# Attention scores and gate logits: one 4-byte product of unsplit operands for three products of split halves

## The chip, the cores and the metric

The kernel runs on one core of a Trainium2 chip, in one launch. The metric is the device time of that launch in microseconds (us). Three timed runs of the kernel before gave 884.1, 889.33 and 892.63 us; the median is 889.33 us. One further run was profiled and took 885.66 us.

The engines are called by the profile's names: PE is TensorE (PEld its loads of weights, the stationary operand), DVE is VectorE, ACT is ScalarE, POOL is GpSimd and SP is SyncE. Each engine takes its instructions in the order in which they were written for it.

## The reference

Three layers follow one another: causal attention with a window of 128 positions and a bias linear in the distance (batch 4, 8 heads, 576 positions, head size 64), a mixture of 8 experts in which each token goes to the one expert with the largest logit, and a gated layer. All of it is in 4-byte floating point.

```python
scores = q @ k.T / sqrt(64)                       # per batch and head
scores = where(0 <= rel < 128, scores - slope[h] * abs(rel), -1e9)
attn = softmax(scores);  x = (attn @ v).reshape(2304, 512)
logits = x @ w_gate + modality_bias[modality_id]  # (2304, 8)
e = argmax(logits);  gate = softmax(logits)[e]
x = gate * (relu(x @ w1[e]) @ w2[e])
xn = x / rms(x) * rms_g
out = (silu(xn @ w_gate2) * (xn @ w_val)) @ w_out
```

The change touches two products: the scores `q @ k.T` and the logits `x @ w_gate`. Which expert a token goes to hangs on the logits' largest entry.

## The kernel before, in words

**Tiles and stages.** The 2304 tokens are 18 tiles of 128. The attention stage, with the gate, fills the first 200 us or so of the span; the expert layer and the gated layer follow, are mostly large products, and are not touched by the change.

**The attention pipeline.** A tile `t` has two half tiles `g`, of four heads each. `attention_step(n)` writes out one step of a pipeline over half tiles: it goes through the table `AT` (lines 800 to 806), whose entries are a name and a lag, and writes the named piece of work for the half tile `n - lag`. The order of the table is therefore the order of each engine's queue; there is no scheduler that moves anything. There are 36 score groups (`qk`), one for each half tile, and the distance from one group to the next is called a step here. Pieces that exist once for a tile are written in every second step.

**The split of scores.** For each tile, `tq` and `tk` transpose q and k on PE (line 180, four transposes of 128x128 each) into a PSUM bank (pool bank "d", two of them). `qhi` and `khi` copy the bank on ACT into `qT[:, 0]` and `kT[:, 0]`, of type F32R, in which a product is one pass with rounded operands (lines 198 and 211). `qlo` and `klo` then write on DVE what the rounding took off, into `qT[:, 1]` and `kT[:, 1]` (lines 202 and 215). `kT` is a ring of three tiles, and the scores of a tile go against its own 128 keys and the 128 before it: 256 columns, or 128 at the start of a batch that begins with a tile (tiles 0 and 9).

**The score products.** `qk` (lines 226 to 251) has two products of heads side by side: head `j = 0` lies in rows 0 to 63 of the operands, head `j = 1` in rows 64 to 127, each with its own PSUM bank (bank "a"). For each of two pairs of heads (`u`) it issues high by high, high by low and low by high, 12 products in a group:

```python
for u in range(2):
    for n, (ql, kl) in enumerate(((0, 0), (0, 1), (1, 0))):
        for j in range(2):
            nc.tensor.matmul(sps[j][:, u, :W], qT[rows, ql, i], win(kl, i, j), ...)
```

`ttr` (line 278, DVE) adds the bias and takes the row's extreme, `exp` (line 289, ACT) the exponential, and in the next step `pt` transposes the result on PE (lines 311 and 319), `pall` and `pcur` copy it (lines 325 and 331 or 334), and a step later `pv` multiplies it by v (lines 354 and 356). The operands of `pv` are F32, not split; in the trace each of its products is recorded as two loads of weights and two matmuls.

**The gate.** `xs` (line 366, DVE) scales a tile's output, `tx` transposes it (line 375), `xhi` (line 380, ACT) and `xlo` (line 385, DVE) split it, and `lg` (lines 391 and 392) issues eight F32R products with the split gate weights `wgr` as the stationary operand and 128 columns. `lT` (line 396, ACT) copies the result, `tl` (line 400, one F32 product with the constant `two`) adds its two halves and turns it, and `gate` (line 407 onward, DVE) reads the logits from the bank `few`. `route`, `place` and an indirect DMA by POOL (line 455, `xd<-xs,pli`) then put the tile's rows in the order of the experts.

**Other work in the stage.** POOL and ACT split the weights of the two largest experts (lines 577 and 578) in the later steps. `choose` (line 459) picks these two experts after tile 4, on DVE.

Of the kernel before, what the change touches and what calls it, by code (L numbers as in the profile page):

```python
# [8 lines left out]
F32 = mybir.dt.float32  # L9
F32R = mybir.dt.float32r  # L10
# [4 lines left out]
AF = mybir.ActivationFunctionType  # L15
ALU = mybir.AluOpType
# [3 lines left out]
P = 128  # L20
B, H, SEQ, DH = 4, 8, 576, 64
# [3 lines left out]
KD = D // P  # L25
E = 8
# [6 lines left out]
R = 3  # L33
# [41 lines left out]
def attn_moe_glu(tc, I, out, dbg=None):  # L75
    nc = tc.nc
    with contextlib.ExitStack() as top:
# [8 lines left out]
        ident = cst.tile([P, P], F32, name="ident")  # L86
# [41 lines left out]
        tail = top.enter_context(tc.tile_pool(name="tail", bufs=2, side="right"))  # L128
        att = contextlib.ExitStack()
        a1 = att.enter_context(tc.tile_pool(name="a1", bufs=1, side="right"))  # L130
        a2 = att.enter_context(tc.tile_pool(name="a2", bufs=2, side="right"))
# [4 lines left out]
        def block_tile(name):  # L136
            return tail.tile([P, D], F32, name=name, tag="block", bufs=2)

        def small(shape, dtype, name, bufs=2):
            return tail.tile(shape, dtype, name=name, tag=name, bufs=bufs)  # L140

        T, QT, G, M, X, RK, CUM = {}, {}, {}, {}, {}, {}, {}
# [9 lines left out]
        load(1, "qk")  # L152
        load(0, "v")
        wg = a1.tile([P, KD, E], F32, name="wg")
        wgr = tail.tile([P, KD, 2 * E], F32R, name="wgr", bufs=1)
        two = tail.tile([2 * E, E], F32, name="two", bufs=1)
        nc.scalar.dma_start(wg, I["moe_w_gate"].rearrange("(k p) e -> p k e", p=P))
        mb = a1.tile([P, 2, E], F32, name="mb")
        mid = a1.tile([P, NT], I32, name="mid")
# [8 lines left out]
        nc.gpsimd.memset(zrow, 0.0)  # L168
        fills = [(xd, r, XW) for r in range(0, OTHER, P)] + [(yd, r, XW) for r in range(0, NTOK, P)]

        kT = a1.tile([P, 2, KD, R * P], F32R, name="kT")
        kTf = kT.bitcast(F32)

        def bank(name, use=None):
            return ps.tile([P, 512], F32, name=use or name, tag=name, bufs=BANKS[name])

        def turn(src, t, use):
            tp = bank("d", use)
            for i in range(KD):
                nc.tensor.transpose(  # L180
                    tp[:, i * P : i * P + P], src[:, 2 * i : 2 * i + 2].rearrange("p h d -> p (h d)"), ident
                )
            return tp.rearrange("p (k x) -> p k x", k=KD)

        def warm(n):

            wt = bank("b", "warm")
            for _ in range(n):
                nc.tensor.matmul(wt, ones, wbf, start=True, stop=True)

        few = bank("e", "few")

        def tq(t):
            QT[t] = a2.tile([P, 2, KD, P], F32R, name="qT", tag="qT"), turn(T["q", t], t, "tq")

        def qhi(t):
            qT, x = QT[t]
            nc.scalar.activation(qT[:, 0], x, AF.Copy, scale=-(DH**-0.5))

        def qlo(t):  # L200
            qT, x = QT[t]
            nc.vector.scalar_tensor_tensor(
                qT[:, 1], x, -(DH**-0.5), qT.bitcast(F32)[:, 0], ALU.mult, ALU.subtract
            )

        def tk(t):
            QT["k", t] = turn(T["k", t], t, "tk")

        def khi(t):
            cs = (t % R) * P  # L210
            nc.scalar.activation(kT[:, 0, :, cs : cs + P], QT["k", t], AF.Copy)

        def klo(t):
            cs = (t % R) * P
            nc.vector.tensor_tensor(
                kT[:, 1, :, cs : cs + P], QT.pop(("k", t)), kTf[:, 0, :, cs : cs + P], ALU.subtract
            )

        def geo(t):
            full = (t * P) % SEQ != 0  # L220
            cs, pr = (t % R) * P, ((t - 1) % R) * P
            swap = full and pr > cs
            oc = 0 if (swap or not full) else P
            return full, cs, pr, swap, oc, P - oc, (2 * P if full else P), (P if (swap or not full) else 0)

        def qk(t, g):
            full, cs, pr, swap, oc, op, W, b0 = geo(t)
            if g == 0:
                M[t] = (a2.tile([P, H], F32, name="mn"), small([P, H], F32, "sm"))
            qT = QT[t][0]  # L230
            lo, hi = min(cs, pr), max(cs, pr)

            def win(hl, i, j):
                rows = slice(DH * j, DH * j + DH)
                if not full:
                    return kT[rows, hl, i, cs : cs + P]
                if hi - lo == P:
                    return kT[rows, hl, i, lo : hi + P]
                k3 = kT[rows, hl, i].rearrange("p (r x) -> p r x", x=P)
                return k3[:, lo // P : hi // P + 1 : (hi - lo) // P]  # L240

            sps = [bank("a", "s").rearrange("p (u x) -> p u x", u=2) for j in range(2)]
            for u in range(2):
                i = 2 * g + u
                for n, (ql, kl) in enumerate(((0, 0), (0, 1), (1, 0))):
                    for j in range(2):
                        rows = slice(DH * j, DH * j + DH)
                        nc.tensor.matmul(  # L248
                            sps[j][:, u, :W], qT[rows, ql, i], win(kl, i, j), start=n == 0, stop=n == 2
                        )  # L250
            G[t, g] = [sps, [], None]

        def parts(t):
# [122 lines left out]
            M[t] = x.rearrange("p (k x) -> p k x", k=KD)  # L376

        def xhi(t):
            hi, lo = (block_tile("xT").bitcast(F32R).rearrange("p (k x) -> p k x", k=KD) for _ in range(2))
            nc.scalar.activation(hi, M[t], AF.Copy)  # L380
            M[t] = hi, lo, M[t]

        def xlo(t):
            hi, lo, x = M[t]
            nc.vector.tensor_tensor(lo, x, hi.bitcast(F32), ALU.subtract)

        def lg(t):
            hi, lo, _ = M.pop(t)
            x = few[: 2 * E, :P]
            for k in range(KD):  # L390
                nc.tensor.matmul(x, wgr[:, k], hi[:, k], start=k == 0, stop=False)
                nc.tensor.matmul(x[:E], wgr[:, k, :E], lo[:, k], start=False, stop=k == KD - 1)

        def lT(t):
            M[t] = small([2 * E, P], F32, "lT")
            nc.scalar.activation(M[t], few[: 2 * E, :P], AF.Copy)

        def tl(t):

            nc.tensor.matmul(few[:, P : P + E], M.pop(t), two, start=True, stop=True)  # L400

        def gate(t):

# [102 lines left out]
            nc.scalar.dma_start(mid, I["moe_modality_id"].bitcast(I32).rearrange("(t p w) -> p t w", p=P, w=2)[:, :, 0])  # L506

        def gating():
            nc.scalar.activation(wgr[:, :, :E], wg, AF.Copy)
            nc.vector.tensor_tensor(wgr[:, :, E:], wg, wgr.bitcast(F32)[:, :, :E], ALU.subtract)  # L510
            nc.vector.scalar_tensor_tensor(
                two, ident[: 2 * E, :E], -1.0, ident[: 2 * E, E : 2 * E], ALU.mult, ALU.subtract
            )

        def scales(c, part):

# [267 lines left out]
        def conversions():  # L784
            gd4 = gd.rearrange("f p (m x) -> p f m x", x=P)
            for fb in range(NFF // 4):
# [7 lines left out]
                for f in range(fb * 4, fb * 4 + 4):  # L794
# [4 lines left out]

        AT = [  # L800
# [4 lines left out]
            ("pcur", 1),  # L805
        ]
        FN = dict(tq=tq, qhi=qhi, qlo=qlo, tk=tk, khi=khi, klo=klo, rs=rs, xs=xs, tx=tx, xhi=xhi, xlo=xlo, lg=lg, lT=lT,
                  tl=tl, gate=gate, gexp=gexp, rk=rk, route=route)
        HALF = dict(qk=qk, pt=pt, pall=pall, pcur=pcur, pprev=pprev, pv=pv)
        for j in range(2):  # L810
            for f in (ttr, exp, mix):
# [4 lines left out]
        def attention_step(n):  # L816
# [3 lines left out]
            if n == 3:  # L820
                modality()
                gating()
# [11 lines left out]
            for name, lag in AT:  # L834
# [21 lines left out]
                elif 0 <= t < NT:  # L856
                    if name in HALF:
                        HALF[name](t, g)
                    elif g == 0:
                        FN[name](t)  # L860
                        if t == 0 and name in WARM:
                            warm(WARM[name])
                if name == "pt" and n in WN:
                    warm(WN[n])

        WARM = dict(tq=0, klo=4, qk=0)
        warm(8)
        last = 2 * NT - 1 + LAG["pv"]
        end = 2 * NT - 2 + LAG["place"]
# [494 lines left out]
        with tc.tile_pool(name="o1", bufs=1, side="left") as o1, tc.tile_pool(name="o2", bufs=2, side="left") as o2:  # L1364
            ot_i, no_i, zero = OVER["rows"], OVER["number"], OVER["zero"]
            n_over = nc.values_load(no_i[0:1, 0:1], min_val=0, max_val=NOVER)
            with tc.For_i(0, n_over, 1) as i:
# [7 lines left out]
                def turned(src, n):  # L1375
                    xT = o1.tile([P, n, P], F32, name=f"xT{n}")
                    for k0 in range(0, n, KD):
                        tx = bank("b", "tx")
                        for k in range(KD):
                            nc.tensor.transpose(  # L1380
                                tx[:, k * P : k * P + P], src[:, (k0 + k) * P : (k0 + k + 1) * P], ident
                            )
                        for k in range(KD):
                            nc.vector.tensor_copy(xT[:, k0 + k], tx[:, k * P : k * P + P])
                    return xT

                xT = turned(xg, KD)
# [62 lines left out]
```

## Time and profile before

| | |
|---|---|
| median of three runs | 889.33 us (884.1 to 892.63) |
| profiled execution, its own time | 885.66 us |
| its span, first to last instruction | 883.9 us |
| PE busy | 839.9 us, 95% |
| PEld busy | 655.6 us, 74% |
| DVE busy | 632.7 us, 72% |
| ACT busy | 413.1 us, 47% |
| POOL busy | 174.6 us, 20% |

Busy time of PE is the time in which at least one of its matmuls is recorded as running; the records of neighbouring matmuls overlap, and their ends are modelled. What a matmul costs the queue is therefore read from the distance between the starts of neighbours. [...]

### The profile page before, as it was taken

Reading aid. Unit: us, or ns where it says so; the run is one execution under the profiler, and the core shown is the slowest. Engines: PE = TensorE matmul, PEld = TensorE weight load, DVE = VectorE, ACT = ScalarE, POOL = GpSimd, SP = SyncE. Lnnn points to the kernel's source line nnn. Section 1 sums busy time; section 2 is a strip of 40 time slices with the busy share of each in tenths; the row PEclk is TensorE's granted clock in tenths of the full one; section 3 lists DMA queues with packets and bytes.
Section 4 is the critical chain, followed back from the end, with each engine's and each line's share of the span. In section 5 each row is a group of like instructions: output and inputs, shape, how many; then the busy total and the mean of one; then the engine's idle time right before and its main releaser. Section 6 shows DMA issues by size and latency. Waiting matters only on the chain.

```text
span 883.9 us, 17689 instructions
## 1 busy us (share of the span) xinstructions
PE 839.9 (95%) x6107; PEld 655.6 (74%) x6107; DVE 632.7 (72%) x1703; ACT 413.1 (47%) x975; POOL 174.6 (20%) x206
## 2 busy tenths in 40 slices
PE   8999988999899999999899999899999999999994
PEld 5978987987788888888765555457877877778882
DVE  7899889899988787543447747766666666767752
ACT  5787678866545545332346535333233233233221
POOL 2564127541443334200000001001001001001001
PEclk9999897999999999999999999999999999999998
DMA  9996379515787776241036106301001000000001
GB/s 192 262 260 138 105 227 268 166 57 185 229 252 223 228 247 209 93 152 40 13 144 226 37 1 239 142 13 61 13 1 49 25 2 36 1 2 27 11 1 38
DMA packets 100472, 101.99 MB, mean 115 GB/s; under 512 B 63136, under 2 KB 75424, under 8 KB 100384
## 3 DMA queue, kind: packets, MB, share of 16 engines
q1 hardware_dynamic: 92848, 86.34, 34.1%
q0 software_dynamic: 4400, 14.20, 4.1%
q8 instruction: 54, 0.88, 0.4%
q10 hardware_dynamic: 3136, 0.30, 0.4%
q14 instruction: 34, 0.28, 0.1%
HBM read 67.18 MB, written 33.89 MB: 114 GB/s over the span
## 4 chain that ended last, share of the span: by engine, by line
PE 67%; DVE 16%; issue 9%; ACT 5%; DMA 2%; POOL 0%; SPq 0%; ACTq 0%; DVEq 0%; POOLq 0%
PE g L1056 12%; PE y L717 11%; PE h L692 11%; PE acc L1170 9%; PE gv L1072 8%; PE s L248 2%; DVE pb L278 2%; PE xp L356 2%; PE xp L354 2%; PE mth L668 2%; PE pt L319 1%; DVE gv L962 1%; ACT gv L961 1%; PE mtx L668 1%; PE gtx L1018 1%
## 5 line engine op out<-in xcount | busy, mean ns | idle before, releaser
L1056 PEld LDWEIGHTS <-gv 128*128 128x128 f16 x2016 | 167.7, 98 | 11.2
L1056 PE MATMUL g<-xc,gv 128*128 128x192 f16 x2016 | 175.0, 246 | 0.0
L745 POOL DMA_INDIRECT out<-o,ix x18 | 18.1, 1003 | 397.5 <-ACT o L1179 394.8
L717 PE MATMUL y<-W,hhi 128*128 x304 | 95.6, 395 | 0.0
L1072 PE MATMUL gv<-xn,gv 128*128 128x384 f16 x528 | 90.6, 326 | 1.6 <-ACT other L1136 0.9
L692 PE MATMUL h<-W,xhi 128*128 x272 | 89.4, 410 | 0.1
L1170 PE MATMUL acc<-go,alo 128*128 128x512 f16 x216 | 81.9, 379 | 0.0
L289 ACT ACTIVATE pb<-pb,mn 128x256 f32<-128x256 f32 (+4 forms) x160 | 74.4, 467 | 12.7 <-DVE mn L278 9.7
L1072 PEld LDWEIGHTS <-gv 128*128 128x128 f16 x528 | 51.6, 98 | 38.2 <-issue 2.6
L1170 PEld LDWEIGHTS <-ahi 128*128 128x128 f16 x432 | 41.3, 98 | 41.6 <-ACT ahi L1131 3.2
L717 PEld LDWEIGHTS y<-W,hhi 128*128 128x128 f32 x304 | 57.0, 188 | 13.9
L1170 PE MATMUL acc<-gv,ahi 128*128 128x512 f16 x216 | 64.3, 379 | 3.2 <-ACT o L1179 1.5
L1170 PE MATMUL acc<-go,ahi 128*128 128x512 f16 x216 | 64.3, 379 | 0.7 <-ACT ahi L1131 0.7
L278 DVE CUSTOM_DVE_ANT_0 pb<-s,bias 128x256 f32<-128x256 f32 (+4 forms) x160 | 53.5, 378 | 10.8 <-PE s L248 9.9
L781 POOL TENSOR_TENSOR cw<-cw,cv 128x512 int32<-128x512 int32 x36 | 47.0, 1309 | 69.8 <-DVE cw L780 31.0
L717 PE MATMUL y<-W,hlo 128*128 x152 | 60.1, 396 | 0.0
L692 PEld LDWEIGHTS h<-W,xhi 128*128 128x128 f32 x272 | 48.9, 191 | 9.9 <-issue 0.4
L692 PE MATMUL h<-W,xlo 128*128 x136 | 54.3, 400 | 0.0
L1136 ACT ACTIVATE one<-one,undo 128x384 f32<-128x384 f32 x24 | 14.8, 615 | 83.2 <-DVE one L1127 82.6
L727 ACT ACTIVATE yn<-y,xg 128x512 f32<-128x512 f32 x19 | 13.1, 688 | 82.6 <-PE y L717 82.6
L1131 ACT ACTIVATE ahi<-one 128x384 f16<-128x384 f32 x36 | 18.8, 523 | 55.7 <-DVE one L1137 55.7
L248 PE MATMUL s<-kT,qT 64*128 64x256 f32 (+1 forms) x432 | 40.7, 312 | 3.4 <-DVE mn L278 1.7
(283 smaller groups left out, 1714.1 us busy)
## 6 DMA issues: line engine op xcount, KB each, us to landing
raw<-gd SPq DMA_DIRECT2D x20, 768.0 KB
gd<-cw SPq DMA_DIRECT2D x36, 256.0 KB
W<-in_moe_w SPq DMA_DIRECT2D x16, 512.0 KB
cv<-in_moe_w_gate SPq DMA_DIRECT2D x12, 512.0 KB
cv<-in_moe_w_val SPq DMA_DIRECT2D x12, 512.0 KB
cv<-in_moe_w_out SPq DMA_DIRECT2D x12, 512.0 KB
xd<-zrow SPq DMA_DIRECT2D x20, 257.0 KB
xg<-xd SPq DMA_DIRECT2D x19, 257.0 KB
```

Source lines behind the costliest of these rows:

```text
L248: nc.tensor.matmul(sps[j][:, u, :W], qT[rows, ql, i], win(kl, i, j), start=n == 0, stop=n == 2)
L278: nc.vector.tensor_tensor_reduce(pb[rw, u, x0:x1], sp[rw, u, x0:x1], bias[rw, h, b0 + x0 : b0 + x1], 1.0, 3.0e38, ALU.add, ALU.min, M[t][0 ...
L289: nc.scalar.activation(pb[rw, u, x0:x1], pb[rw, u, x0:x1], AF.Exp, bias=mn[rw, h : h + 1], scale=-1.0, accum_out=sm[rw, h : h + 1],)
L668: nc.tensor.transpose(tx[:, k * P : k * P + P], src[:, (k0 + k) * P : (k0 + k + 1) * P], ident)
L692: nc.tensor.matmul(hp[f], x[:, k], WT[1][k][:, ds(w, 1), part, f * 512 : f * 512 + 512], start=k == 0 and n == 0, stop=k == KD - 1 and n == 2,
L717: nc.tensor.matmul(y, x[:, k], WT[2][k // 2][:, ds(w, 1), part, k % 2 * D : k % 2 * D + D], start=k == 0 and x is hi and part == 0, stop=k ...
L745: return nc.gpsimd.indirect_dma_start(dst[:, :], bass.IndirectOffsetOnAxis(ap=ix[:, 0:1], axis=0), src, None, bounds_check=NTOK - 1, oob_i ...
L781: nc.gpsimd.tensor_tensor(ci, ci, low.bitcast(I32), ALU.add)
L1056: nc.tensor.matmul(acc[:, gv * HT : gv * HT + HT], GV[p][:, a, gv, i, m * P : m * P + P], XC[c][:, b, j, m], start=m == 0 and n == 0, stop ...
L1072: nc.tensor.matmul(acc[:, :CHT], w[:, m * P : m * P + P], XC[c][b][:, k], start=k == 0 and n == 0, stop=k == KD - 1 and n == 2,)
L1131: nc.scalar.activation(ahi, si, AF.Copy, scale=2.0**-LOW)
L1170: nc.tensor.matmul(acc, a[:, cols], GO[f][part], start=f == 0 and n == 0, stop=f == NFF - 1 and n == 2,)
```

## The change

The low halves go. `qT` and `kT` become F32 and hold one copy each, `qlo`, `klo` and `xlo` are removed, and a score is one F32 product: 4 in a group in place of 12, now written pair of heads by pair of heads. For the gate, `xhi` makes one F32 copy, and `lg` issues four F32 products with that copy as the stationary operand and the gate's 8 columns (negated, `wgn`) as the moving one; the logits land in `few` in the shape in which `gate` reads them, so that `lT` and `tl` are removed. The four matmuls that are issued after `klo` in the first step are issued after `khi`.

```diff
-        wgr = tail.tile([P, KD, 2 * E], F32R, name="wgr", bufs=1)
-        two = tail.tile([2 * E, E], F32, name="two", bufs=1)
+        wgn = tail.tile([P, KD, E], F32, name="wgn", bufs=1)
...
-        kT = a1.tile([P, 2, KD, R * P], F32R, name="kT")
-        kTf = kT.bitcast(F32)
+        kT = a1.tile([P, KD, R * P], F32, name="kT")
...
-            nc.scalar.activation(qT[:, 0], x, AF.Copy, scale=-(DH**-0.5))
-
-        def qlo(t):
-            qT, x = QT[t]
-            nc.vector.scalar_tensor_tensor(
-                qT[:, 1], x, -(DH**-0.5), qT.bitcast(F32)[:, 0], ALU.mult, ALU.subtract
-            )
+            nc.scalar.activation(qT, x, AF.Copy, scale=-(DH**-0.5))
...
-            nc.scalar.activation(kT[:, 0, :, cs : cs + P], QT["k", t], AF.Copy)
-
-        def klo(t):
-            cs = (t % R) * P
-            nc.vector.tensor_tensor(
-                kT[:, 1, :, cs : cs + P], QT.pop(("k", t)), kTf[:, 0, :, cs : cs + P], ALU.subtract
-            )
+            nc.scalar.activation(kT[:, :, cs : cs + P], QT.pop(("k", t)), AF.Copy)
...
-                for n, (ql, kl) in enumerate(((0, 0), (0, 1), (1, 0))):
-                    for j in range(2):
-                        rows = slice(DH * j, DH * j + DH)
-                        nc.tensor.matmul(
-                            sps[j][:, u, :W], qT[rows, ql, i], win(kl, i, j), start=n == 0, stop=n == 2
-                        )
+                for j in range(2):
+                    rows = slice(DH * j, DH * j + DH)
+                    nc.tensor.matmul(sps[j][:, u, :W], qT[rows, i], win(i, j), start=True, stop=True)
...
-            hi, lo = (block_tile("xT").bitcast(F32R).rearrange("p (k x) -> p k x", k=KD) for _ in range(2))
-            nc.scalar.activation(hi, M[t], AF.Copy)
-            M[t] = hi, lo, M[t]
-
-        def xlo(t):
-            hi, lo, x = M[t]
-            nc.vector.tensor_tensor(lo, x, hi.bitcast(F32), ALU.subtract)
+            x = block_tile("xT").rearrange("p (k x) -> p k x", k=KD)
+            nc.scalar.activation(x, M[t], AF.Copy)
+            M[t] = x
...
-                nc.tensor.matmul(x, wgr[:, k], hi[:, k], start=k == 0, stop=False)
-                nc.tensor.matmul(x[:E], wgr[:, k, :E], lo[:, k], start=False, stop=k == KD - 1)
-
-        def lT(t):
-            M[t] = small([2 * E, P], F32, "lT")
-            nc.scalar.activation(M[t], few[: 2 * E, :P], AF.Copy)
-
-        def tl(t):
-
-            nc.tensor.matmul(few[:, P : P + E], M.pop(t), two, start=True, stop=True)
+                nc.tensor.matmul(few[:, P : P + E], x[:, k], wgn[:, k], start=k == 0, stop=k == KD - 1)
...
         AT = [
             ("tq", -2), ("mix1", 1), ("gexp", 8), ("qhi", -2), ("rk", 8), ("xhi", 5), ("khi", -1), ("ttr0", 0),
-            ("ttr1", 0), ("lg", 6), ("lT", 6), ("ws", -1), ("qlo", -2), ("exp0", 0), ("route", 8), ("weights", 11),
-            ("mix0", 0), ("klo", -1), ("tl", 7), ("tx", 4), ("pt", 1), ("pall", 1), ("exp1", 0), ("xlo", 5),
+            ("ttr1", 0), ("lg", 6), ("ws", -1), ("exp0", 0), ("route", 8), ("weights", 11),
+            ("mix0", 0), ("tx", 4), ("pt", 1), ("pall", 1), ("exp1", 0), 
```

On PE, in two steps in the first third of the stage, the queue reads as follows before (`s` the scores, `tk` and `tq` the transposes of k and q, `few` the gate's bank, `pt` the transposes of the exponentials, `xp` the products with v, of which a group has eight):

```order
L248 MATMUL s<-kT,qT 128x256 x12
L180 MATMUL tk<-ident,kn 128x128 x4
L400 MATMUL few<-two,lT 128x8
L311 MATMUL pt<-ident,pb 128x128 x4
L354 MATMUL xp<-vn,pc 128x64
L356 MATMUL xp<-vn,pa 128x64
...
L248 MATMUL s<-kT,qT 128x256 x12
L180 MATMUL tq<-ident,qn 128x128 x4
...
L391 MATMUL few<-xT,wgr 16x128
L392 MATMUL few<-xT,wgr 8x128
```

The same place with the change:

```order
L233 MATMUL s<-kT,qT 128x256 x4
L178 MATMUL tk<-ident,kn 128x128 x4
L294 MATMUL pt<-ident,pb 128x128 x4
L337 MATMUL xp<-vn,pc 128x64
L339 MATMUL xp<-vn,pa 128x64
...
L233 MATMUL s<-kT,qT 128x256 x4
L178 MATMUL tq<-ident,qn 128x128 x4
...
L369 MATMUL few<-wgn,xT 128x8 x4
```

The score group keeps its place with 4 products for 12, the product between `tk` and `pt` is gone, and the 8 products of `lg` are 4.

On DVE, in two steps at the same place, before (the `L278` rows with `pb,mn<-s,bias` are the work on the scores of one head, `oh` the gate's choice, `xs` the scaled output, `pc` a copy of `pt`):

```order
L278 ISA pb,mn<-s,bias 128x192
...
L202 SCALAR_TENSOR_TENSOR qT<-tq,qT 128x512
L431 TENSOR_SCALAR s_861<-s_861 128x1
...
L331 TENSOR_TENSOR pc<-pt,mcur 128x512
L278 ISA pb,mn<-s,bias 128x192
...
L215 TENSOR_TENSOR kT<-tk,kT 128x4x128
L385 TENSOR_TENSOR xT<-tx,xT 128x512
```

With the change:

```order
L261 ISA pb,mn<-s,bias 128x192
...
L400 TENSOR_SCALAR s_746<-s_746 128x1
...
L314 TENSOR_TENSOR pc<-pt,mcur 128x512
L261 ISA pb,mn<-s,bias 128x192
...
L376 ISA l,s_884<-few,MB 128x8
```

The three passes over 512 columns of a tile are gone from DVE's queue, and nothing else there changes its order.

## Rows read from the trace of the kernel before

**Rows 1.** The page: busy time of the engines, and the granted clock in 40 slices of the span.
```profile
PE 839.9 (95%) x6107; PEld 655.6 (74%) x6107; DVE 632.7 (72%) x1703; ACT 413.1 (47%) x975; POOL 174.6 (20%) x206
...
PEclk9999897999999999999999999999999999999998
```
**Rows 2.** Busy time by stretch: start:end, length, engines (instructions), granted clock, DMA share, GB/s.
```profile
56.00:83.20 27.20, 26.91 (x267) 24.57 (x265) 25.86 (x97) 21.42 (x75) 15.98 (x24) 1.00 0.92 205
83.20:102.30 19.10, 17.21 (x138) 15.76 (x137) 15.13 (x78) 10.64 (x40) 3.29 (x5) 0.82 0.30 76
120.80:139.50 18.70, 15.19 (x152) 13.91 (x151) 14.69 (x52) 13.28 (x42) 5.09 (x6) 1.00 1.05 306
139.50:156.40 16.90, 14.66 (x99) 13.77 (x98) 15.13 (x55) 14.79 (x48) 14.06 (x19) 0.70 0.84 270
```
**Rows 3.** PE in order of time: start, us to the last end, line, operation, count.
```profile
120.76 0.98 PE L248 MATMUL s<-kT,qT 64*128 64x256 f32 x12
121.67 0.66 PE L180 MATMUL tq<-ident,qn 128*128 128x128 f32 x4
122.16 0.17 PE L426 MATMUL few<-oh,upper 128*128 128x8 bf16 x1
...
122.22 0.22 PE L391 MATMUL few<-xT,wgr 128*16 128x128 f32 x1
...
122.63 0.22 PE L392 MATMUL few<-xT,wgr 128*8 128x128 f32 x1
...
126.51 0.39 PE L356 MATMUL xp<-vn,pa 128*128 128x64 f32 x2
126.73 0.39 PE L354 MATMUL xp<-vn,pa 128*128 128x64 f32 x2
...
129.08 0.66 PE L180 MATMUL tk<-ident,kn 128*128 128x128 f32 x4
...
129.98 1.09 PE L319 MATMUL pt<-ident,pb 128*128 128x128 f32 x8
130.91 0.33 PE L354 MATMUL xp<-vn,pa 128*128 128x64 f32 x2
```
**Rows 4.** PE in order of time, a score group of 128 columns.
```profile
98.22 0.88 PE L248 MATMUL s<-kT,qT 64*128 64x128 f32 x12
99.04 0.66 PE L180 MATMUL tk<-ident,kn 128*128 128x128 f32 x4
```
**Rows 5.** By tile: durations in ns (min/median/max), first and last start.
```profile
L248 PE MATMUL s<-kT,qT x432: 269/278/579, 7.1 to 187.9; 64*128 64x256 f32 x128, 64*128 64x128 f32 x16
L354 PE MATMUL xp<-vn,pa x88: 220/275/421, 15.3 to 197.8; 128*128 128x64 f32 x88
L391 PE MATMUL few<-xT,wgr x72: 218/222/308, 32.0 to 205.5; 128*16 128x128 f32 x72
```
**Rows 6.** The chain that ended last, in order of time: start, us, what.
```profile
6.87 0.60 DVE qT L202
7.46 0.61 DVE kT L215
8.12 0.77 PE s L248 x10
...
156.43 0.91 PE s L248 x12
...
166.07 0.91 PE s L248 x12
...
180.23 0.60 DVE xT L385
...
187.21 0.96 PE s L248 x10
```
**Rows 7.** DVE in order of time: start, us, line, operation, and waits in brackets.
```profile
124.22 0.69 DVE L366 TENSOR_TENSOR xs<-xp,rs 128x512 f32<-128x512 f32 x1 [3.55 <-DMA xd<-xs,pli]
...
132.43 3.20 DVE L414 SCALAR_TENSOR_TENSOR oh<-rev,s,sgn 128x8 bf16<-128x8 f32 x1
```

More of the change, by code (lines that the diff above doesn't have):

```diff
@@ L193, in tq @@
         def tq(t):
-            QT[t] = a2.tile([P, 2, KD, P], F32R, name="qT", tag="qT"), turn(T["q", t], t, "tq")
+            QT[t] = a2.tile([P, KD, P], F32, name="qT", tag="qT"), turn(T["q", t], t, "tq")
         def qhi(t):
             qT, x = QT[t]
-            nc.scalar.activation(qT[:, 0], x, AF.Copy, scale=-(DH**-0.5))
-        def qlo(t):
-            qT, x = QT[t]
-            nc.vector.scalar_tensor_tensor(
-                qT[:, 1], x, -(DH**-0.5), qT.bitcast(F32)[:, 0], ALU.mult, ALU.subtract
-            )
+            nc.scalar.activation(qT, x, AF.Copy, scale=-(DH**-0.5))
         def tk(t):
@@ L231, in qk, with win @@
             lo, hi = min(cs, pr), max(cs, pr)
-            def win(hl, i, j):
+            def win(i, j):
                 rows = slice(DH * j, DH * j + DH)
                 if not full:
-                    return kT[rows, hl, i, cs : cs + P]
+                    return kT[rows, i, cs : cs + P]
                 if hi - lo == P:
-                    return kT[rows, hl, i, lo : hi + P]
-                k3 = kT[rows, hl, i].rearrange("p (r x) -> p r x", x=P)
+                    return kT[rows, i, lo : hi + P]
+                k3 = kT[rows, i].rearrange("p (r x) -> p r x", x=P)
                 return k3[:, lo // P : hi // P + 1 : (hi - lo) // P]
@@ L378, in xhi @@
         def xhi(t):
-            hi, lo = (block_tile("xT").bitcast(F32R).rearrange("p (k x) -> p k x", k=KD) for _ in range(2))
-            nc.scalar.activation(hi, M[t], AF.Copy)
-            M[t] = hi, lo, M[t]
-        def xlo(t):
-            hi, lo, x = M[t]
-            nc.vector.tensor_tensor(lo, x, hi.bitcast(F32), ALU.subtract)
+            x = block_tile("xT").rearrange("p (k x) -> p k x", k=KD)
+            nc.scalar.activation(x, M[t], AF.Copy)
+            M[t] = x
         def lg(t):
-            hi, lo, _ = M.pop(t)
-            x = few[: 2 * E, :P]
+            x = M.pop(t)
             for k in range(KD):
-                nc.tensor.matmul(x, wgr[:, k], hi[:, k], start=k == 0, stop=False)
-                nc.tensor.matmul(x[:E], wgr[:, k, :E], lo[:, k], start=False, stop=k == KD - 1)
-        def lT(t):
-            M[t] = small([2 * E, P], F32, "lT")
-            nc.scalar.activation(M[t], few[: 2 * E, :P], AF.Copy)
-        def tl(t):
-            nc.tensor.matmul(few[:, P : P + E], M.pop(t), two, start=True, stop=True)
+                nc.tensor.matmul(few[:, P : P + E], x[:, k], wgn[:, k], start=k == 0, stop=k == KD - 1)
         def gate(t):
@@ L508, in gating @@
         def gating():
[L509 to L513, printed above, removed]
+            nc.scalar.activation(wgn, wg, AF.Copy, scale=-1.0)
         def scales(c, part):
@@ L806, in attn_moe_glu @@
         ]
-        FN = dict(tq=tq, qhi=qhi, qlo=qlo, tk=tk, khi=khi, klo=klo, rs=rs, xs=xs, tx=tx, xhi=xhi, xlo=xlo, lg=lg, lT=lT,
-                  tl=tl, gate=gate, gexp=gexp, rk=rk, route=route)
+        FN = dict(tq=tq, qhi=qhi, tk=tk, khi=khi, rs=rs, xs=xs, tx=tx, xhi=xhi, lg=lg,
+                  gate=gate, gexp=gexp, rk=rk, route=route)
         HALF = dict(qk=qk, pt=pt, pall=pall, pcur=pcur, pprev=pprev, pv=pv)
@@ L864, in attention_step @@
                     warm(WN[n])
-        WARM = dict(tq=0, klo=4, qk=0)
+        WARM = dict(tq=0, khi=4, qk=0)
         warm(8)
```

## The prediction

> **What bounds the kernel now.** I began with the page [rows 1]: PE is busy 95% of the span. That says little by itself, since everything after the attention stage is large products that the change leaves alone. The change touches the first 200 us or so, so that is where I looked, and there the question is which queue ends each of the 36 steps. A step begins where a score group begins.
>
> The chain of waits gives steps in which nothing holds PE up: from 156.43 to 166.07 us there are two, of 4.82 us each [rows 6]. The stretch from 56 to 83.2 us holds six in 27.2 us, 4.53 each, with PE busy nearly throughout at the full clock [rows 2]. Such steps are simply PE's queue, one piece behind the other. Others are longer. From 83.2 to 102.3 there are three steps in 19.1 us, at a mean granted clock of 0.82; from 120.8 to 139.5 three in 18.7; from 139.5 to 156.4 two in 16.9, at 0.70 [rows 2]. Set against 4.53 or 4.82 these stretches lose 5.5, 4.2 and 7.3 us. [...] DVE is late for its own reasons too: it waited 3.55 us for a transfer of placed rows to let go of a buffer, and one small instruction took 3.20 us [rows 7].
>
> So the stage changes between two limits: PE's queue, and DVE a little behind it. The change makes PE's queue longer and DVE's shorter.
>
> **What goes.** DVE loses three passes for each of 18 tiles, 54 of 0.60 us: 32 us of its work. Only those on the chain can count: qT, kT and xT passes stand there 25 times, the first at 6.87 and the last at 180.23 us, together 14.8 us [rows 6]. That is the upper bound of what DVE gives back. The lower bound is nothing, if PE's queue is right behind each of them. In the first 27 us little else is ready, and five of the passes with 3.1 us stand there, the first two directly ahead of the first group of scores [rows 6]; I take all of that. Of the other 11.7 us I take four fifths, because the long stretches lose 17 us in all and the passes stand in them. Together **-12.5 us**. ACT loses one small copy for each tile, which I cost at nothing: it stands beside PE's transposes, and in the stretches shown ACT is less busy than DVE.
>
> On PE the product of `tl` goes. From `tk` to `pt` the queue takes 0.90 us, from `tq` to the next piece, with four transposes alone between, 0.49 [rows 3]: 0.41 for each tile, **-7.4 us**.
>
> **What comes: the scores.** A group of 12 split products takes 0.91 us from its first start to the next piece [rows 3]. Its last product starts 0.70 us after the first (0.98 less the 0.28 of one product [rows 5]). [...] I read six turns of two, 0.117 us each, and 0.21 us around them.
>
> What an unsplit product of 256 columns costs, this trace does not show. The nearest rows are those of `xp`: unsplit, 64 columns, two records for each product, 0.22 us from one product to the next, 0.11 for a record [rows 3].
> - Upper bound: the 0.11 us is all columns. Then 256 columns take 0.446 us a record.
> - Lower bound: the 0.11 is all loading of weights, as in the score group of 128 columns, which takes 0.82 us against 0.91 and has turns of 0.10 us although its columns are half as many [rows 3, 4]. Then a record costs no more than a split product's turn, 0.117.
> - Between: the shortest record of `xp`, with 64 columns, lasts 220 ns, and a split product of 128 columns in `few` 218 [rows 5]. A transpose of 128 unsplit columns takes 0.93 / 8 = 0.116 us, where split products of 128 columns follow each other every 0.059 (seven distances in 0.41 us) [rows 3]. [...] I take **0.225 us**, the value that two independent rows give.
>
> The order within a group decides the rest. Head 0 now issues both its records before head 1 issues any. A head's second record has to wait until its first has gone through the same rows, but head 1's first record can run beside it. So the eight records take five turns: 5 x 0.225 + 0.21 = 1.34 us, 0.43 more than 0.91. For 32 groups that is **+13.6 us**; the four groups of 128 columns have five turns of 0.10 in place of six, -0.4.
>
> [...]
>
> **What comes: the logits.** Four unsplit products with 8 columns and 128 columns of weights are eight records. Their columns hardly matter; I take `xp`'s 0.11 us a record, 0.88 us. Eight split ones take 0.47 (0.41 to the last start and one distance) [rows 3]. That is **+7.4 us** for 18 tiles. Bounds: 0.10 a record gives +5.9, a record as long as a whole one stands alone, 0.22 us, +23; records follow each other in the queue, so the low end is the nearer one.
>
> **Sum.** +13.6 - 0.4 + 7.4 - 7.4 - 12.5 = **+0.7 us**. Everything after the stage stays. The profiled execution took 885.66 us and lies 3.7 us under the median of the runs; with the same difference the median is 889.33 + 0.7 = **890 us**. This case's own range is 882 to 898: DVE's return between 5 and 15 us, a record between 0.213 and 0.236.
>
> **Rivals.**
> - *The heads of a pair run in series.* The written order is the place: two records of one head stand next to each other, and if head 1's first record does not start until head 0's second is through, a group has eight turns: 8 x 0.225 + 0.21 = 2.01 us, +1.10 for 32 groups, +35, and +0.8 for the four short ones. PE would then end every step, and DVE would return its full 14.8 us: 889.3 + 35 + 1 - 15 = **910 us**. It decides from the point at which a group costs 0.4 us more than now (12.5 us over 32 groups). For it: the trace shows pairs side by side only where they are written alternately. [...]
>   [...]
> - *A record costs what `xp`'s columns would make it,* 0.446 us: 5 x 0.446 + 0.21 = 2.44 us, +49, less 15: **923 us**. The 220 ns of `xp`'s shortest record speaks against it.
> - *PE waits for nothing any more.* If DVE's relief also spares PE the stretch at the lower clock, the return is 14.8 and the 7.3 us lost from 139.5 to 156.4, and 2 us of the wait on the transfer: 24 in place of 12.5, **878 us**. For it: the clock was down just where DVE had been late. Against it: the transfer and the 3.20 us instruction are not touched by the change.
> - *A record is as cheap as a split product,* 0.117 us: 5 x 0.117 + 0.21 = 0.80 us, -3.5 for 32 groups, and -12.5: **873 us**. The transposes speak against it.
>
> That the change does not do what it says is excluded by the order of PE's queue: 4 products stand for 12, and the three passes are gone from DVE's.
>
> **How the numbers follow.** One per cent, about what a measurement can tell from no change, is 8.9 us: 880.4 to 898.2. Chances: the forecast 54%, series 22%, the dear record 5%, no waits 13%, the cheap record 6%. Of the forecast I put a twentieth below and a fourteenth above that band; of the case without waits two thirds below. Faster: 2.7 + 9 + 6 = 18%. Slower: 4 + 22 + 5 = 31%. Same: 51%. The range 876 to 910 leaves out the dear and the cheap record, part of the series, and little else.
>
> **What would show it.** In the profile after: a score group of 256 columns from first start to the next piece of 1.34 us (2.0 for series, 2.4 for the dear record, 0.8 for the cheap one); starts of the two heads' records in pairs; the gate's group at 0.9; steps of about 5.2 us without a gap on PE; DVE's busy time down by 30 us or more; the clock from 139 to 156 us. The forecast is wrong if the group takes over 1.8 us, or if steps stay long although DVE is idle, which would mean that ACT or POOL ends them.

## The result, and the profile after

The changed kernel takes **874.7 us** (median of 6 runs, 873.45 to 880.13); the kernel before, run beside it, 887.14 (884.1 to 892.63). The ratio is **0.9858 [0.9826, 0.989]**: faster by 1.4%, 12.4 us by the medians. Runs that lie more than 1.5% above the fastest of their kernel are left out of all ratios. Forecast were 890 us and a range of 876 to 910, so the time lies just under the range. The profiled execution took 880.13 us, 5.4 above its median and 5.5 below the profiled one of before; its span is 878.3 us.

The page answers to [rows 1]:

```profile
PE 839.8 (96%) x5927; PEld 652.4 (74%) x5927; DVE 594.4 (68%) x1647; ACT 408.4 (47%) x957; POOL 175.2 (20%) x206
...
PEclk9969989999999999999999999999999999999998
```

DVE's busy time falls by 38.3 us: a pass is recorded for 0.68 to 0.69 us, of which the next instruction overlaps the last 0.08, so the 54 passes are 37 us of busy time and 32 us of the queue's. PE's busy time is the same to 0.1 us. The scores end earlier: by tile, their last product starts at 181.5 us against 187.9 [rows 5], so the 5.5 us between the two spans come from the attention stage.

What the products cost shows on PE in order of time, the columns as in [rows 3]; first groups of 256 columns and the gate's, then one of 128 columns as in [rows 4]:

```profile
160.49 1.14 PE L233 MATMUL s<-kT,qT 64*128 64x256 f32 x8
161.55 0.66 PE L178 MATMUL tk<-ident,kn 128*128 128x128 f32 x4
162.05 1.04 PE L302 MATMUL pt<-ident,pb 128*128 128x128 f32 x8
...
164.75 1.13 PE L233 MATMUL s<-kT,qT 64*128 64x256 f32 x8
165.81 0.66 PE L178 MATMUL tq<-ident,qn 128*128 128x128 f32 x4
...
166.36 1.04 PE L369 MATMUL few<-wgn,xT 128*128 128x8 f32 x8
167.25 0.63 PE L358 MATMUL tx<-ident,xs 128*128 128x128 f32 x4
...
95.06 0.71 PE L233 MATMUL s<-kT,qT 64*128 64x128 f32 x8
95.71 0.66 PE L178 MATMUL tk<-ident,kn 128*128 128x128 f32 x4
```

A score group takes 161.55 - 160.49 = 1.06 us to the next piece; 0.91 before, 1.34 forecast. The short group takes 0.65, 0.82 before. The gate's eight records take 0.89, as forecast (0.88). Between `tk` and `pt` there are 0.50 us where `tl` made it 0.90. By tile, in ns as in [rows 5]:

```profile
L233 PE MATMUL s<-kT,qT x288: 272/376/792, 6.6 to 181.5; 64*128 64x256 f32 x128, 64*128 64x128 f32 x16
L369 PE MATMUL few<-wgn,xT x144: 175/256/361, 28.0 to 197.3; 128*128 128x8 f32 x144
```

There are 288 records for 144 products, two for each, as `xp`'s had let expect; the split products, of type F32R, had one each (432 for 36 groups of 12 [rows 5]). Single records of the first group above start at 160.488 and 160.495 (the two heads), 160.808 and 160.815, 161.024 and 161.031, 161.240 and 161.247 us: four turns of both heads, 0.216 us from turn to turn after a first of 0.32.

The traces show two levels of the granted clock, 1.00 and 0.50 of the full one: in the kernel before, every microsecond from 90 to 96 us has 0.50 and every one from 97 to 102 us has 1.00. A mean such as 0.83 is over both. The stage by stretch, cut where score groups begin as in [rows 2], with its columns:

```profile
6.64:22.60 15.96, 14.53 (x113) 11.63 (x113) 12.20 (x59) 13.63 (x51) 5.75 (x8) 1.00 1.02 240
45.48:60.98 15.50, 15.50 (x79) 13.68 (x78) 6.05 (x30) 9.43 (x35) 6.96 (x13) 0.56 1.09 281
60.98:70.04 9.06, 9.06 (x79) 8.16 (x78) 6.11 (x29) 6.07 (x21) 4.51 (x7) 1.00 0.76 192
84.30:98.50 14.20, 13.56 (x122) 12.28 (x121) 10.47 (x65) 9.27 (x34) 2.56 (x4) 1.00 0.37 91
116.10:139.00 22.90, 18.15 (x139) 16.51 (x138) 13.05 (x52) 14.03 (x44) 7.32 (x9) 0.85 0.90 275
139.00:150.50 11.50, 10.66 (x87) 9.07 (x86) 8.98 (x48) 11.13 (x36) 9.42 (x15) 1.00 1.02 316
150.54:160.49 9.95, 9.95 (x88) 9.02 (x87) 6.12 (x33) 9.95 (x34) 8.20 (x10) 1.00 0.99 307
```

The kernel before, in the same steps as the first three and the last of these rows:

```profile
7.05:27.05 20.00, 17.51 (x133) 14.65 (x132) 15.87 (x66) 13.27 (x49) 5.24 (x8) 0.83 1.26 230
49.95:60.45 10.50, 9.47 (x89) 8.21 (x88) 10.22 (x39) 9.53 (x35) 6.90 (x13) 1.00 1.04 263
60.45:69.22 8.77, 8.77 (x89) 8.16 (x88) 8.06 (x31) 6.73 (x25) 5.00 (x8) 1.00 1.11 255
156.36:166.00 9.64, 9.64 (x97) 9.04 (x96) 8.34 (x32) 7.62 (x25) 5.60 (x8) 1.00 0.80 237
```

Where PE is busy without a gap at the full clock in both kernels, two steps (one tile) take 9.06 us in place of 8.77, and 9.95 in place of 9.64: PE's part did become dearer, by 0.3 us for a tile. The first five steps take 15.96 us in place of 20.00. The three steps that took 19.10 us at a clock of 0.82 take 14.20 at full clock, and the two that took 16.90 at 0.70 take 11.50 at full clock: **10.3 us come back in these five steps**.

Two stretches are worse. The two steps from 45.48 to 60.98 us take 15.50 us in place of 10.50: they run mostly at the lower level (a mean clock of 0.56, and 0.50 in every microsecond from 46 to 59 us), with PE busy throughout. This belongs to this execution and not to the change: a second profile of the same kernel (the run that repeats the change, below) has the same two steps at the full clock, in 5.4 us less.

```profile
46.35:56.46 10.11, 9.49 (x80) 8.15 (x79) 6.04 (x30) 8.84 (x32) 6.45 (x12) 1.00 1.07 277
```

The 38.8 us of steps ahead of these two agree to 0.02 us in the two profiles, so PE had done the same work before the clock fell in the one and not in the other. 5.4 us is also what the profiled execution has above its median.

The other stretch is one of three steps: 18.70 us before, 22.90 now. What holds it up shows on DVE and then on PE, in order of time, waits in brackets as in [rows 7]:

```profile
122.50 0.69 DVE L349 TENSOR_TENSOR xs<-xp,rs 128x512 f32<-128x512 f32 x1 [7.18 <-DMA xd<-xs,pli]
```
```profile
123.24 1.12 PE L358 MATMUL tx<-ident,xs 128*128 128x128 f32 x4 [4.46 <-DVE xs L349]
```

The wait for the transfer of placed rows has doubled (3.55 us in [rows 7]), and PE stands behind it. It is also in the chain of waits (start, us, what), where its 7.41 us are the longest piece between 84 and 150 us:

```profile
113.06 0.41 DVE pb L261
113.48 0.34 DVE pb L261
113.82 0.34 DVE pb L261
114.17 0.34 DVE pb L261
...
114.99 7.41 DMA xd<-xs,pli
...
122.50 0.70 DVE xs L349
```

Elsewhere it is now mostly DVE that waits. What it waited for in the first 206 us (total us, times, longest):

```profile
DVE pb L261 <- PE s L233: 22.5, 15, 4.0
DVE xs L349 <- DMA xd<-xs,pli: 7.2, 1, 7.2
```

Before, the first of these was 9.9 us. The stage is now mostly PE's, but for one transfer.

### The profile page after: what moved, and what is told of

Read it like the earlier page. It is cut to its first block, busy times and chain, and to the rows that moved or that the text cites. A ratio compares the mean times of both kernels' runs of the same rounds, so it can differ in the third digit from the quotient of the medians.

```text
span 878.3 us, 17260 instructions
## 1 busy us (share of the span) xinstructions
PE 839.8 (96%) x5927; PEld 652.4 (74%) x5927; DVE 594.4 (68%) x1647; ACT 408.4 (47%) x957; POOL 175.2 (20%) x206
## 3 DMA queue, kind: packets, MB, share of 16 engines
q0 software_dynamic: 4400, 14.20, 4.2%
## 4 chain that ended last, share of the span: by engine, by line
issue 43%; PE 41%; DVE 8%; DMA 3%; ACT 2%; POOL 1%; POOLq 0%; SPq 0%; ACTq 0%; DVEq 0%
PE h L657 10%; PE y L682 10%; PE s L233 3%; PE g L1021 3%; PE xp L337 3%; PE xp L339 2%; DVE pb L261 2%; PE acc L1135 2%; PE mth L633 1%; PE few L369 1%; PE pt L302 1%; POOL out L710 1%; DMA yd<-yn,ix 1%; PE mtx L633 1%; DMA xd<-xs,pli 1%
## 5 line engine op out<-in xcount | busy, mean ns | idle before, releaser
L1101 ACT ACTIVATE one<-one,undo 128x384 f32<-128x384 f32 x24 | 14.8, 615 | 83.7 <-DVE one L1092 83.7
L692 ACT ACTIVATE yn<-y,xg 128x512 f32<-128x512 f32 x19 | 13.1, 690 | 84.1 <-PE y L682 84.1
```

## The experiments

Three questions were open after the result: which of the parts brings the gain, why a score group costs 1.06 us, and whether the wait for the transfer can be removed. Ratios are against the kernel before, run on the same chip; T1 and T2 are the two theories of the expectation.

**The scores alone.** The change, with the split products of the gate put back, and with them `xlo`, `lT` and `tl`:

```diff
-            for k in range(KD):
-                nc.tensor.matmul(few[:, P : P + E], x[:, k], wgn[:, k], ...)
+            for k in range(KD):
+                nc.tensor.matmul(x, wgr[:, k], hi[:, k], start=k == 0, stop=False)
+                nc.tensor.matmul(x[:E], wgr[:, k, :E], lo[:, k], start=False, stop=k == KD - 1)
...
```

> Scores by unsplit products, gate logits split as before. Theory 1 (the DVE passes give back about 17 us in all, a third for each of the three kinds; a score group costs PE 0.15 us more in 32 steps, the gate costs PE nothing): +4.4 - 11.3, so about 880 us against 887. Theory 2 (the gain is PE's own: fewer matmul records in the score group and none of the passes matters): the whole gain, about 875 us.

Measured: 881.72 us, 0.9911 [0.988, 0.9942]. The scores, with 36 of the 54 passes, bring 0.9%, some 7 us, as T1 had it.

**The logits alone.** The kernel before with `xhi` and `lg` of the change, so without `xlo`, `lT` and `tl`:

> Gate logits by unsplit products, scores split as before. Theory 1: one of three DVE passes goes and PE's queue stays as long as it was (the four unsplit products take 0.9 us, the eight split ones and the turning product took as much): -5.7 us, about 881. Theory 2: the score group is as before, so about 887, no change.

Measured: 889.82 us, 0.9986 [0.9934, 1.0038]. T1's 881 was wrong: the gate's part alone does nothing that can be told from no change. The two parts together make 0.9897, the whole change 0.9858; with these intervals that is no proof that they help each other.

**Before, without the passes.** Three split products remain, but they read the high halves in place of the low ones, and the three passes are not computed (the low parts are left out of the result):

```diff
-                for n, (ql, kl) in enumerate(((0, 0), (0, 1), (1, 0))):
+                for n, (ql, kl) in enumerate(((0, 0), (0, 0), (0, 0))):
...
-            nc.vector.tensor_tensor(lo, x, hi.bitcast(F32), ALU.subtract)
+            return
```

> The kernel before, without the three DVE passes that write the low halves: the products read the high halves in their place, so PE's queue has the same products (the output differs from the reference). Theory 1: DVE's relief comes without PE's price, 887 - 17 = about 870 us, a little faster than the changed kernel. Theory 2: the passes do not matter, about 887.

Its two fastest runs took 877.18 and 877.67 us, its other two 891.8 and 896.84: too few for a ratio. The kernel before had 888.53; by the fast two that is -11, not the -17 that T1 wanted. With PE's products as they were, DVE's relief brings no more than the whole change does, as far as two runs can say. A wait on DVE shows what may hold it up:

```profile
118.55 0.69 DVE L362 TENSOR_TENSOR xs<-xp,rs 128x512 f32<-128x512 f32 x1 [8.85 <-DMA xd<-xs,pli]
```

Its `xs` begins at 118.55 us; the second profile of the change has it at 117.05. The shorter queue of PE ahead of this point bought nothing there.

**The change, with three idle passes.** Each pass is put back at its old place in DVE's queue, and its output is read by nobody:

```diff
+        def idle_pass(x, y):
+            z = a2.tile([P, KD, P], F32, name="idl", tag="idl")
+            nc.vector.tensor_tensor(z, x, y, ALU.subtract)
```

> The changed kernel with three DVE passes of the old size at the old places in the queue, into scratch that nobody reads. Theory 1: DVE's relief is taken back and PE's price stays, 874.7 + 17 = about 892 us, slower than the kernel before. Theory 2: as the changed kernel, about 875.

Measured: 889.27 us, 1.0015 [0.9981, 1.0049]: T1's side, far from T2's 875. **The whole gain is the passes**; their removal is worth 1.0015 - 0.9858 = 1.6%, 14 us, uncertain by 4. All the rest of the change costs 1.3 us with an uncertainty of 3. By tile, in ns, an idle pass takes what the old one took (the first line is the kernel before):

```profile
L202 DVE SCALAR_TENSOR_TENSOR qT<-tq,qT x18: 678/686/692, 6.8 to 174.3; 128x512 fp32r<-128x512 f32 x18
L200 DVE TENSOR_TENSOR idl<-tq,qT x18: 677/686/692, 6.8 to 179.0; 128x512 f32<-128x512 f32 x18
```

No product waits for what an idle pass writes, so the passes cost time as work in DVE's queue, not because the scores wait for the low halves. They also hold their PSUM bank longer, which is a rival cause; in this run's trace PE waits for an idle pass to let go of a bank only twice, 0.8 us together.

**The order within a score group.** Forecast were five turns because of the written order. Here the heads are written one wholly after the other:

```diff
-            for u in range(2):
-                i = 2 * g + u
-                for j in range(2):
+            for j in range(2):
+                for u in range(2):
+                    i = 2 * g + u
```

> The changed kernel with the four products of a score group written head by head (both pairs of head 0, then both of head 1) instead of alternately. Theory A (records of two neighbouring products are laid side by side only where the products use different halves of the rows, so the middle two products pair and the outer two do not): six turns of 0.216 us and 0.2, a group of 1.5 us in place of 1.06; +0.44 in 32 groups, +14, about 885 us after waits give some back. Theory B (each half of the rows has a queue of its own, with room for at least four records): the group stays at 1.06 and the time at 875.

Measured: 874.73 us, 0.9872 [0.9804, 0.9939], as the change; PE in order of time has a group of 1.08 us:

```profile
154.89 1.14 PE L233 MATMUL s<-kT,qT 64*128 64x256 f32 x8
155.97 0.66 PE L178 MATMUL tk<-ident,kn 128*128 128x128 f32 x4
```

The group stays nearly as it was, 1.08 us in place of 1.06, as theory B had it; A (1.5 us a group, 885 us in all) falls. The records still start in pairs, 154.894 and 154.907, 155.214 and 155.227, and so on. What lets them, a queue for each half of the rows or something else, the trace does not show.

**Both heads in one half of the rows.** The operands of head 1 are read from the rows of head 0 (so half of the scores are other ones):

```diff
-                rows = slice(DH * j, DH * j + DH)
+                rows = slice(0, DH)
```

> The changed kernel, with both heads of a pair read from rows 0 to 63 of the operands (the scores of head 1 are those of head 0, so the output is not the reference's). Theory A (a turn is 0.216 us for one record's 256 columns, and two turns stand side by side only because the heads lie in different halves of the rows): eight turns, 8 x 0.216 + 0.2 = 1.93 us a group, +0.87 in 32 groups and +0.4 in each of four, +29 less what waits give back, about 895 to 905 us. Theory B (the eight records of a group run one after the other, 0.11 us each, bound by the loads of their weights, and which rows they use does not matter): the group stays at 1.06 us and the time at 875.

Measured: 893.51 us, 1.002 [0.9982, 1.0057], and PE in order of time:

```profile
164.06 1.99 PE L233 MATMUL s<-kT,qT 64*128 64x256 f32 x8
165.99 0.66 PE L178 MATMUL tq<-ident,qn 128*128 128x128 f32 x4
```

1.93 us, 0.87 more than in two halves: four more turns of 0.217, as A had it. So a turn takes 0.216 to 0.217 us in both runs, and the records ran side by side only where the heads lay in two halves of the rows. The 0.87 us for 32 groups and 0.43 for four (a group of 128 columns takes 1.08 us here, 0.65 in two halves) add 29.6 us to PE's queue, but the time grows by 1.6%, some 15 us, a little under A's range: about half is absorbed, in waits that PE had. The mean granted clock is 0.983 to 0.992 over its ten runs, against 0.981 to 0.989 over the six of the change.

**The transfer.** Four more changes aim at the 7.18 us wait. In the first, three more tiles of `xs` get room of their own, so that `xs` waits for no transfer:

```diff
-            x = t1.tile([P, XW], F32, name=f"xs{t}") if t <= T0 else row_tile("xs")
+            x = (t1 if t <= T0 else a1).tile([P, XW], F32, name=f"xs{t}") if t <= T0 + 3 else row_tile("xs")
```

> The changed kernel with room for three more tiles of scaled rows (tiles 5 to 7 take theirs from the attention pool, in the room that the smaller kT leaves), so that xs of tile 10 need not wait until the rows of tile 5 have been placed. Theory 1 (DVE's relief runs into that wait and a part of it is given back there): PE's wait of 4.5 us in the changed kernel's trace goes, and the lower clock after it; 874.7 - 4.5 to 874.7 - 8, about 867 to 870 us. Theory 2 (the wait is only moved: another transfer or POOL ends the step): 873 to 876.

Measured: 879.81 us, 0.9912 [0.9877, 0.9946]: not faster, if anything slower. DVE's wait is gone, but some 15 us later PE stands 9.22 us for a memset on POOL:

```profile
138.32 1.97 PE L302 MATMUL pt<-ident,pb 128*128 128x128 f32 x8 [9.22 <-POOL pb L257]
```

POOL in order of time shows why: its queue holds the placing, which itself waits for the same transfers, and the splitting of the expert weights ahead of the memset:

```profile
134.16 1.00 POOL L424 DMA_INDIRECT xd<-xs,pli  x1 [2.41 <-DMA xd<-xs,pli]
135.19 2.48 POOL L543 TENSOR_TENSOR W<-W 128x512 fp32r<-128x512 f32 x2
...
137.86 0.77 POOL L257 MEMSET pb<- 64x384 f32 x2
```

T2's reading holds, the wait moved, though the time is above its 873 to 876. The same with the three idle passes:

> The same three tiles of rows, and three idle DVE passes of the old size at the old places. Theory 1: without the wait on the transfer the passes cost more than the 14.6 us that they cost with it, since no wait hides a part of them: e5 + 18, about 886 us. Theory 2 (the wait hides nothing): e5 + 14 or less, about 882.

Measured: 890.83 us, 1.003 [0.9997, 1.0062], 11 us over the run without them: the passes cost about the same here, which again is T2's side.

Then half as many loads of expert weights until step 28, alone and with the room for rows:

```diff
-                        for _ in range(2):
+                        for _ in range(1 if n < 28 else 2):
```

> The changed kernel, with one load of expert weights in a step in place of two up to step 27. Theory 1 (the wait in the middle of the stage is the placing of rows, queued behind 4 MB of expert weights that SP issues in the same steps): the placing lands in some 4 us in place of 6 to 7, PE's wait before tx goes from 4 us to under 2, 3 to 4 us faster than the changed kernel beside it, about 871. Theory 2 (the wait only moves to the splits of the weights, which come later now, on ACT and POOL): the same time or up to 5 us slower.

> As the run before it, with three more tiles of rows as in the run with more rows. Theory 1: neither xs nor POOL waits for a placing that is queued behind weights, 5 to 8 us faster than the changed kernel, about 868. Theory 2: POOL's queue still ends a step, as with more rows alone, and the time is that of the changed kernel, 875 to 880.

Measured: 877.76 us, 0.9864 [0.9802, 0.9927], and 881.09, 0.9902 [0.9862, 0.9942]. `xs` still waits 6.1 us for the transfer in the first; in the second PE waits 6.3 us for the memset. And three placings in a step in place of two:

```diff
-                        for x in waiting[:2]:
+                        for x in waiting[:3]:
```

> The changed kernel, with three tiles of rows placed in a step in place of two after the two experts are chosen, so that tile 5 is placed before the expert weights are loaded. Theory 1: xs of tile 10 finds its buffer free or nearly so, 3 to 4 us faster, about 871. Theory 2: the loads start earlier by the same step and the wait is as long, no change.

Measured: 875.49 us, 0.9827 [0.9764, 0.9889], which is no different from the change itself, run again beside these three:

> The changed kernel once more, as the measure for the three next to it. Both theories: 873 to 880 us, its time hanging on how long PE ran at the lower clock.

Measured: 877.95 us, 0.9853 [0.9784, 0.9922]. `xs` waits 7.4 us with three placings, 6.23 in this second profile of the change. No version here is shown to beat the change.

## Why the prediction was wrong

- **The step that failed is the score term on PE, "eight records take five turns".** Its record price was right (0.225 taken, 0.216 measured), its count of turns was not: four, with a record of each head starting together in either written order (160.488 and 160.495 us alternately, 154.894 and 154.907 head by head). No run shows the 0.225 us, or the 0.213 and 0.236 of the range; they were my estimates, and the turns measured 0.216 us (0.217 in one half). A group costs 0.15 us more than before, not 0.43: 32 x 0.15 = +4.8 us in place of +13.6. This 8.8 us is most of the 12.4 + 0.7 = 13.1 us by which the forecast missed (the 890 us are 2.2 us further off, because the kernel before took 887.14 when it was run beside the change). Of the signs named for being wrong, a group over 1.8 us did not come, and a group between 0.80 and 1.34 was not thought of; steps that stay long while DVE is idle came in one stretch, but a transfer ended them, not ACT or POOL. The error is in an assumption on order that no row carried; the rows had pairs side by side only where they were written alternately, and I let that decide. The two heads stand in different rows in either case, and that was the fact that mattered: a group takes 1.06 and 1.08 us in two halves, 1.93 in one.
- **The short groups**: -0.17 us each, -0.7 (forecast -0.4). **The logits**: 0.89 - 0.47 = +0.42 for a tile, +7.6 (forecast +7.4). **`tl`**: 0.90 - 0.50 = 0.40, as forecast. With these PE's queue grows by 4.8 - 0.7 + 7.6 - 7.4 = 4.3 us; for a tile of two long groups they make 2 x 0.15 + 0.42 - 0.40 = 0.32, and the steps without a gap on PE show 0.29 and 0.31. The run with idle passes has 1.3 us, uncertain by 3, so the 4.3 are just within it.
- **What DVE gives back**: 14 us, uncertain by 4, against 12.5 forecast and an upper bound of 14.8. The size was right, and so was the start of the stage, where 4.0 us came back (3.1 forecast); for the rest it was luck in part. The chain lists 24 passes, not 25 (their 14.8 us stand), and "the passes stand in them" does not hold for the long stretches: these five are all that do, 3.2 us of the other 11.7 (the chain of the kernel before, as in [rows 6]):

```profile
100.37 0.69 DVE kT L215
101.06 0.60 DVE xT L385
...
130.65 0.60 DVE kT L215
131.25 0.60 DVE xT L385
...
139.63 0.69 DVE qT L202
```

The two stretches that gave back 10.3 us hold three of them, 2.0 us. What came back there is mostly not the passes' own time: both stretches had the lower clock and run at the full one now. The third long stretch gave nothing back and became 4.2 us longer.

- With only the score terms corrected, the sum would have been 4.3 - 12.5 = -8.2 us, 881. The other 4 us are within the uncertainty of the two terms that remain: DVE's return is 1.5 more, and PE's price need not be paid in full, as the one-half run shows on a larger scale (half of 29.6).
- **The rivals.** The cheap record named 873 us, nearest to the time, by luck: its group of 0.80 us is excluded by the 1.06, as are series (2.01) and the dear record (2.44). The rival without waits named 878. It had the clock right from 139 to 156 us (0.70 before, 1.00 now), but not the whole mechanism: it took 2 us off the wait on the transfer, which grew from 3.55 to 7.18, and attempts to remove it only moved it. With the passes gone from either kernel, `xs` comes to it early and waits (7.18 us in the change, 8.85 in the kernel before without them).
- **The loads of weights** run beside the records. In the changed kernel a load begins 2 ns after a record starts (160.808 and 160.810 us) and lasts 187 ns, in a turn of 216. In the one-half run all score records lie in rows 0 to 63, and there too a load begins 2 ns after a record starts (164.384 and 164.386), with turns of 0.217 us.
- **What stays open**: how much of the 14 us is the clock itself. Over 64 runs of the kernel before, on three chips, the time goes with the time spent at the lower clock, 0.34 us for each us (correlation 0.91; the latter worked out as 2 x (1 - mean clock) x span). The change's ten runs have on average about 22 us less of it, so some 7 us. That is a relation between runs, argued and not isolated; whether the waiting brings about the lower clock or the clock the waiting is not shown. The two profiles of the change come nearest to isolating it: the same steps at a clock of 0.56, which by the same formula are 13.6 us at the lower level, took 5.4 us more. They show what the lower clock costs there, not why removing the passes makes it rarer.

## What to carry to other kernels

Before counting products by the order they are written in, look at which rows of the array each one uses: products in different halves ran side by side here in either order (1.06 and 1.08 us a group, against 1.93 in one half). Ask of every microsecond added to an engine whether it stood waiting in that stretch: PE's 29.6 us more in the one-half run cost 15, DVE's 32 us less returned 14. And look at a wait on a transfer that grows when its waiter gets faster (from 3.55 to 7.18 us here) as a candidate for the next limit; giving it another buffer moved the wait, as 9.22 us on PE, to the next queue that depended on the same transfer. One profile is one execution: compare a second one before you put a stretch down to the change, as the 5.4 us from 45.48 us on show.

## What was not expected of the hardware

Records of products in different row halves started side by side even when they were not neighbours in the written order. In the kernel before the two heads' records are neighbours, and a pair mostly starts 3 ns apart (120.763 and 120.766 us); in the change one record is written between them, and it is 7 ns (160.488 and 160.495); written head by head, three are written between, with their loads, and it is 13 ns (154.894 and 154.907). That is some 3 ns for each place in the written order. The group takes 1.08 us written head by head, 1.06 alternately and 1.93 in one half. So within a group records did not always start in the written order: written head by head, the fifth record, head 1's first, starts at 154.907 us, and the second at 155.214. The trace does not name a record's head; which one it is follows from the pairs, and from their absence in the run in one half. The first turn of a group takes 0.32 us and the later ones 0.216.
